# Softmax exponentials on VectorE: a cubic in four steps replaced by four integer mantissa readings that TensorE sums

## Chip, cores, metric

One core of a Trainium2 chip. The metric is the device time of one execution in microseconds (us). Every run lists the clock that TensorE was granted.

## The reference, cut to what matters

Two transformer layers, each an attention block and a feed-forward block, in bf16. Per layer 32 heads of width 16 look over 2048 tokens, so there are 2 x 32 x 2048 x 2048 exponentials. In tiles of 128 keys by 512 queries that is 4096 tiles. The two layers are the lines marked `A` below.

```python
def _A_ref(x, wqkv, wo):
    B, S, D = x.shape            # 1, 2048, 512
    H = 32; Dh = D // H
    ...
    scores = jnp.einsum("bhqd,bhkd->bhqk", q, k) * scale
    p = _softmax(scores, axis=-1)
    o = jnp.einsum("bhqk,bhkd->bhqd", p, v)
    ...
x = x + _A_ref(_layernorm(x, axis=-1), A_wqkv, A_wo)
x = x + _B_ref(_layernorm(x, axis=-1), B_w1, B_b1, B_w2, B_b2)   # gelu feed-forward, F = 1376
x = x + _A_ref(...); x = x + _B_ref(...)
```

## The kernel before: the parts that matter

The Python program is a list scheduler: it assigns each operation a guessed duration, decides in what order each engine gets its instructions, and writes that fixed order out with semaphores.

Scores come in groups of three and two tiles in turn (PSUM banks 0 to 2 and 3, 4), which ScalarE exponentiates with one instruction each. Beside a group, one more tile may go to bank 5 (`DLANE`), for VectorE:

```python
            grp = []
            while len(grp) < G:
                self.advance()
                if self.cur == len(self.segs):
                    break
                sg = self.segs[self.cur]
                grp.append((sg, sg["todo"].pop(0)))
            dt = self.take_d() if wide else None
            ...
            for k, (sg, j) in enumerate(grp + ([dt] if dt else [])):
                ops.append(self.score(sg, j, banks[k] if k < len(grp) else DLANE))
            ...
```

Whether there is such a tile is decided here; `lane_busy` is set when a tile is taken and cleared when its load out of bank 5 has been put into VectorE's order:

```python
    def take_d(self):

        self.advance()
        if self.lane_busy or self.cur == len(self.segs) or self.P.free["dve"] - self.S_.now > 1.3:
            return None
        ... (not in a segment's last DTAIL tiles; keys, queries there)
        if self.batch is None:
            p = self.S_.pools["dt"]
            if not p.free:
                return None
            self.batch = {"slot": p.free.pop(0), "tiles": [], "loaded": 0, "closed": False}
        self.lane_busy = True
        sg["todo"].pop(0)
        return (sg, j)

```

VectorE then computes the exponential of two tiles with four instructions, two of which read two tensors (`...` stands for their writes and guessed durations):

```python
    def job_d(self, bt):
        ...
        E,  in0=lo,  scalar=65536.0, in1=lo, op0=subtract, op1=mult        # scalar_tensor_tensor
        v,  in0=lo,  scalar1=..., scalar2=..., op0=mult, op1=add           # tensor_scalar
        D,  in0=E,   in1=v, op=mult                                        # tensor_tensor
        Pb, in0=t32, scalar=2.0 ** -9, in1=D, op0=mult, op1=subtract       # scalar_tensor_tensor
```

TensorE sums P·V of four heads at a time, in four column groups (`tile_position=(0, 32 * hp)`), and makes the scores in four row groups (`tile_position=(32 * hp, 0)`). Where the scheduler predicts a gap on TensorE of more than 0.35 us, it puts filler there, matmuls with zero weights, for 80% of the gap:

```python
FILL_GAP = 0.35
FILL_F = 0.8
    def fill_pe(self, gap):

        P = self.P
        t0 = P.free["pe"]
        n = int(FILL_F * (gap - 0.15) / FILL_T)
        if n < 1:
            return
        n = min(n, 60)
        ...
```

## Time and profile before

| | before |
|---|---|
| median of its runs | 1829.3 us (1827.3 to 1831.2) |
| ScalarE busy | 1741.9 us, 95% of the profiled span |
| VectorE busy | 1593.4 us, 87% |
| TensorE, filler included | 1702.4 us, 93% |
| tiles exponentiated by ScalarE / VectorE | 3635 / 461 |

How to read the lines in the prediction: a group's line names source line, engine, operation and shapes, then the count; after the first bar the busy time and the mean nanoseconds of one; after the second bar how long the engine stood idle just before them, and what ended that. The chain is followed back from the last instruction; its shares tell which engine's work or order set the end. In a view in order of time the first number is the start, the second the duration, and the bracket is an idle stretch and what ended it.

### The profile page before, as it was taken

To read this page: it belongs to the slowest core of one execution; us is meant where nothing else is said; L and a number is where in the kernel's file an instruction comes from. 1 tells how busy PE (TensorE), PEld (TensorE's weight loads), DVE (VectorE), ACT (ScalarE), POOL (GpSimd) and SP (SyncE) were. 2 spreads that over 40 slices of the span, in tenths; PEclk is the share of its full clock that TensorE was granted. 3 is DMA by queue.
4 is the path that set the end of the run, shared out by engine and by line. 5 is a ranking of instruction groups with operands and counts; after the bars stand their busy time and mean duration, and the time that the engine had idled before them with its cause. 6 is when DMAs were issued, how large, how long until landed. Compare 5 with 4: busy or idle time off the path is not lost.

```text
span 1827.5 us, 34039 instructions
## 1 busy us (share of the span) xinstructions
PE 1702.4 (93%) x13894; PEld 658.9 (36%) x13894; DVE 1593.4 (87%) x2516; ACT 1741.9 (95%) x1545; POOL 172.9 (9%) x328
## 2 busy tenths in 40 slices
PE   6989899999999999999999999999999999999998
PEld 2233333333333333333333333333333333333344
DVE  7789989997898999979988899887898798998885
ACT  5989999999999999999999999999999999999996
POOL 4122221100100110002000022100000000000000
PEclk9999999999999999999999999999999999999999
DMA  6551000100100110003500120000000000000000
GB/s 164 97 114 32 24 21 10 36 13 24 56 18 4 44 40 4 18 8 87 85 20 18 19 52 19 13 16 18 7 5 18 11 9 4 4 19 11 18 9 7
DMA packets 146400, 54.63 MB, mean 30 GB/s; under 512 B 131047, under 2 KB 140104, under 8 KB 146248
## 3 DMA queue, kind: packets, MB, share of 16 engines
q1 hardware_dynamic: 146248, 52.46, 12.6%
q8 instruction: 113, 1.85, 0.4%
q14 instruction: 39, 0.32, 0.1%
HBM read 8.69 MB, written 15.30 MB: 13 GB/s over the span
## 4 chain that ended last, share of the span: by engine, by line
ACT 58%; PE 34%; DVE 5%; DMA 2%; issue 1%; POOL 1%; SPq 0%; DVEq 0%; POOLq 0%
ACT PT L979 54%; PE ps L1005 10%; PE ps L1113 6%; PE ps L914 4%; PE ps L750 4%; PE ps L1235 3%; PE ps L1270 3%; PE ps L1203 3%; ACT h L1263 2%; DMA xnT<-xn 1%; DVE dt L990 1%; ACT L979 1%; ACT L1263 1%; DVE de L1064 1%; DVE de L1067 0%
## 5 line engine op out<-in xcount | busy, mean ns | idle before, releaser
L979 ACT ACTIVATE PT<-ps 128x1024 bf16<-128x1024 f32 (+1 forms) x1467 | 1666.2, 1287 | 52.8 <-PE ps L1005 48.5
L1005 PE MATMUL ps<-QT,KT 32*128 32x512 bf16 (+1 forms) x4608 | 605.3, 358 | 92.6 <-ACT PT L979 69.4
L914 PE MATMUL ps<-wqkv,zw 128*128 128x256 bf16 x3269 | 488.3, 276 | 0.0
L1113 PE MATMUL ps<-PT,V 128*17 128x512 bf16 (+1 forms) x4086 | 437.7, 361 | 3.6 <-DVE accT L1143 3.2
L990 DVE TENSOR_SCALAR dt<-ps 128x512 int32<-128x512 f32 x461 | 316.0, 686 | 135.1 <-PE ps L1005 131.7
L1005 PEld LDWEIGHTS ps<-QT,KT 32*128 32x128 bf16 x4608 | 171.8, 91 | 510.0 <-issue 295.3
L914 PEld LDWEIGHTS ps<-wqkv,zw 128*128 128x128 bf16 x3269 | 269.4, 98 | 196.2 <-issue 166.0
L1064 DVE SCALAR_TENSOR_TENSOR de<-dt 128x1024 bf16<-128x1024 uint16 (+1 forms) x243 | 282.2, 1163 | 2.1
L1067 DVE SCALAR_TENSOR_TENSOR de<-dt,dv 128x1024 uint16<-128x1024 int32 (+1 forms) x243 | 281.1, 1160 | 1.8
L1113 PEld LDWEIGHTS ps<-PT,V 128*17 128x17 bf16 x4086 | 108.9, 87 | 238.1 <-issue 204.1
L1066 DVE TENSOR_TENSOR dv<-de,dv 128x1024 f16<-128x1024 bf16 (+1 forms) x243 | 158.6, 655 | 2.0
L1065 DVE TENSOR_SCALAR dv<-dt 128x1024 bf16<-128x1024 uint16 (+1 forms) x243 | 159.7, 660 | 0.0
L1113 PE MATMUL ps<-de,V 128*17 128x512 bf16 (+1 forms) x522 | 137.3, 359 | 1.9 <-DVE accT L1143 0.9
L686 POOL TENSOR_SCALAR rs<-mv 128x4 f32<-128x4 f32 (+2 forms) x19 | 10.9, 572 | 967.1 <-DVE mv L679 966.8
L1235 PE MATMUL ps<-yT,w 128*128 128x512 bf16 (+3 forms) x396 | 97.1, 359 | 1.7 <-DMA yT<-xn 0.7
L750 PE MATMUL ps<-wqkv,xnT 128*128 128x512 bf16 x336 | 94.1, 386 | 4.6 <-DMA xnT<-xn 3.9
L1270 PE MATMUL ps<-w,h 128*128 128x512 bf16 x300 | 80.0, 382 | 0.4 <-ACT g L1264 0.2
L1143 DVE STREAM_TRANSPOSE accT<-ps 128x512 f32<-128x512 f32 (+1 forms) x88 | 58.3, 662 | 15.8 <-PE ps L1113 13.9
L1257 DVE TENSOR_SCALAR h<-ps,b1c 128x512 f32<-128x512 f32 (+2 forms) x88 | 61.8, 702 | 7.8 <-PE ps L1235 7.4
L1203 PE MATMUL ps<-wo,OT 128*128 128x512 bf16 x240 | 66.5, 383 | 0.2
L1183 DVE STREAM_TRANSPOSE OT<-ob 128x512 bf16<-128x512 bf16 (+1 forms) x72 | 46.0, 640 | 0.0
L1113 PEld LDWEIGHTS ps<-de,V 128*17 128x17 bf16 x522 | 32.2, 87 | 38.2 <-issue 29.5
(135 smaller groups left out, 768.8 us busy)
## 6 DMA issues: line engine op xcount, KB each, us to landing
q_scr<-qk SPq DMA_DIRECT2D x22, 256.0 KB, 2.0
k_scr<-qk SPq DMA_DIRECT2D x12, 256.0 KB, 2.0
q_scr<-h SPq DMA_DIRECT2D x10, 256.0 KB, 2.2
out_dram<-xres SPq DMA_DIRECT2D x16, 128.0 KB, 1.7
v_scr<-vst SPq DMA_DIRECT2D x12, 136.0 KB, 1.9
V<-v_scr SPq DMA_DIRECT2D x8, 204.0 KB, 4.6
wqkv<-in_A_wqkv_dram SPq DMA_DIRECT2D x3, 512.0 KB, 4.7
qraw<-q_scr SPq DMA_TRANSPOSE x87, 2.6
```

The lines of the kernel that those rows point to most:

```text
L750: yield Task("pe", prio, [I(lambda e, c=c: e.matmul(self.ps[:, b, :], lhsT=xnT[:, c, :], rhs=self.wqkv[:, c, which * 512:which * 512 + 512 ...
L914: P.op("pe", lambda e: e.matmul(self.ps[:, b, 0:w], lhsT=self.zw[:, :], rhs=rhs, start=st, stop=st, skip_group_check=True), [("zw",), R], ...
L979: S_.submit(Task("act", 1e-5 * gi, [I(lambda e, pt=pt, n=n, b0=b0: e.activation(out=self.PT[:, pt:pt + n, :], in_=self.ps[:, b0:b0 + n, :] ...
L990: S_.submit(Task("dve", 0.0, [I(lambda e, ds=ds, w=w: e.tensor_scalar(out=self.dt32[:, ds, w * 512:(w + 1) * 512], in0=self.ps[:, DLANE, : ...
L1005: return [I(lambda e, kb=kb, i=i: e.matmul(self.ps[:, b, i * W:(i + 1) * W], lhsT=self.KT[32 * hp:32 * hp + 32, hg, kb * 128:(kb + 1) * 12 ...
L1064: yield Task("dve", pr(), [I(lambda e: e.scalar_tensor_tensor(out=E, in0=lo, scalar=65536.0, in1=lo, op0=ALU.subtract, op1=ALU.mult), RT, ...
L1065: yield Task("dve", pr(), [I(lambda e: e.tensor_scalar(out=v, in0=lo, scalar1=CUB_B * sc / 65536.0, scalar2=CUB_A * sc, op0=ALU.mult, op1= ...
L1066: yield Task("dve", pr(), [I(lambda e: e.tensor_tensor(out=D, in0=E, in1=v, op=ALU.mult), [("de", es), ("dv", s)], [("dv", s)], 0.12 + 0.5 ...
L1067: yield Task("dve", pr(), [I(lambda e: e.scalar_tensor_tensor(out=Pb, in0=t32, scalar=2.0 ** -9, in1=D, op0=ALU.mult, op1=ALU.subtract), R ...
L1113: ops.append((i, I(lambda e, hp=hp, hg=hg, kb=kb, ap=ap[:, i * W:(i + 1) * W], first=first and i == 0, W=W: e.matmul(self.ps[32 * hp:32 * ...
L1235: yield Task("pe", pr, [I(lambda e, c=c: e.matmul(self.ps[0:M, b, off:off + W], lhsT=self.w1[:, c, fc * 128:fc * 128 + M], rhs=self.yT[:, ...
L1270: yield Task("pe", pr, [I(lambda e, fc=fc, i=i, b=b: e.matmul(self.ps[:, b, :], lhsT=self.gt(fc, i, W), rhs=self.w2[:, fc, :], start=(fc = ...
```

## The change

Its intent is to make a VectorE tile cheap. The bits of a bf16 number, read as an integer, are nearly linear in its logarithm; so adding a constant to the scaled score and storing it as a 16-bit integer gives a rough exponential, linear within each octave. The change makes four such readings, a quarter of an octave apart, and averages them: P·V is done once per reading, with copies of V multiplied by 1, 2^-1/4, 2^-1/2, 2^-3/4 (rounded). GpSimd makes the copies. To have them at hand, VectorE may only take five fixed key blocks of the 16. The space comes from the feed-forward buffer, f32 before and bf16 now.

```diff
-CUB_A = 38.926064531505304
-CUB_B = 10.143351058007678
+SHIFT = (0, 32, 64, 96)
+WSHIFT = (1.0, 0.83984375, 0.70703125, 0.59375)
+BITS0 = 127.0 * 128.0 - 263.2355
+DK = (3, 6, 9, 12, 15)
-DTAIL = 16
+DTAIL = 8
 ... (buffers: dp 3 x 4 x 1024 U16 and vs for dt32, dv, de; h16 for h32; one vst for two)
+    def job_vs(self, sg, i, kbs):          # GpSimd: weighted copies of V
+        ...
+        yield Task("pool", 0.8, [I(lambda e, k=k: e.tensor_scalar(out=self.vs[:, q, k - 1, i:i + n, :], in0=src, scalar1=WSHIFT[k], ...) for k in (1, 2, 3)])
 ...
-                grp.append((sg, sg["todo"].pop(0)))
+                grp.append((sg, (sg["todo"] or sg["todod"]).pop(0)))
 ...
-                ... tensor_scalar(out=self.dt32[...], in0=self.ps[:, DLANE, :], scalar1=512.0, scalar2=127.0 * 65536.0, op0=mult, op1=add)
+                ... tensor_scalar(out=self.dp[:, ds, 0, ...], in0=self.ps[:, DLANE, :], scalar1=BITS0, scalar2=None, op0=add)
 ... (take_d: from the list todod of the five key blocks)
-        j = sg["todo"][0]
+        j = sg["todod"][0]
+        sg["n"] += len(SHIFT) - 1
 ... (job_d: the four steps go)
+        for k in range(1, len(SHIFT)):
+            yield Task("dve", pr, [I(lambda e, k=k: e.tensor_scalar(out=self.dp[:, s, k, 0:N], in0=self.dp[:, s, 0, 0:N], scalar1=float(SHIFT[k]), scalar2=None, op0=ALU.add), ...)])
+            self.d_ready(bt, k, range(n))
 ... (P·V: the weighted copy where a reading k > 0 is summed)
+                    if sh:
+                        v, RV = self.vs[:, q, sh - 1, d, 17 * hp:17 * hp + 17], ("vs", q, d)
```

## The prediction

> **What bounds the kernel now.** I read the page's busy table first, then the costliest groups (with shapes kept apart), the chain that ended last, the list of waits, and two stretches of TensorE in order of time.
>
> ```profile
> PE 1702.4 (93%) x13894; PEld 658.9 (36%) x13894; DVE 1593.4 (87%) x2516; ACT 1741.9 (95%) x1545; POOL 172.9 (9%) x328
> ACT 58%; PE 34%; DVE 5%; DMA 2%; issue 1%; POOL 1%; SPq 0%; DVEq 0%; POOLq 0%
> ```
>
> ScalarE is busy 95% of the span, VectorE 87%. TensorE's 93% misleads, as the groups show; still, the chain (second line) runs through TensorE for 34% of the span, so TensorE's in-order stream is nearly co-critical.
>
> ```profile
> L979 ACT ACTIVATE PT<-ps 128x1536 bf16<-128x1536 f32 x701 | 1058.6, 1510 | 28.6 <-PE ps L1005 25.8
> L979 ACT ACTIVATE PT<-ps 128x1024 bf16<-128x1024 f32 x766 | 824.7, 1083 | 24.1 <-PE ps L1005 22.7
> L990 DVE TENSOR_SCALAR dt<-ps 128x512 int32<-128x512 f32 x461 | 316.0, 686 | 135.1 <-PE ps L1005 131.7
> L1064 DVE SCALAR_TENSOR_TENSOR de<-dt 128x1024 bf16<-128x1024 uint16 x218 | 265.0, 1216 | 2.0
> L1067 DVE SCALAR_TENSOR_TENSOR de<-dt,dv 128x1024 uint16<-128x1024 int32 x218 | 264.4, 1214 | 1.4
> L1065 DVE TENSOR_SCALAR dv<-dt 128x1024 bf16<-128x1024 uint16 x218 | 149.4, 687 | 0.0
> L1066 DVE TENSOR_TENSOR dv<-de,dv 128x1024 f16<-128x1024 bf16 x218 | 148.0, 680 | 1.7
> L914 PE MATMUL ps<-wqkv,zw 128*128 128x256 bf16 x3269 | 488.3, 276 | 0.0
> ```
>
> Softmax has 4096 score tiles of 128x512. ScalarE exponentiates 701x3 + 766x2 = 3635 of them, VectorE 461. The page gives the ScalarE line (forms together) 1666.2 us busy: 0.458 us a tile. A VectorE tile costs the load, 0.686, and four steps: on the page 282.2 + 281.1 + 159.7 + 158.6 = 881.6 us over 461 tiles, 1.91 us; together 2.60 us. That is 1198 of VectorE's 1593 us; 395 us is other work. L914 is filler, matmuls on zero weights put into predicted gaps; its 488 us is TensorE's slack.
>
> ```profile
> 909.64 0.27 PE L914 MATMUL ps<-wqkv,zw 128*128 128x256 bf16 x1
> 910.00 0.40 PE L1005 MATMUL ps<-QT,KT 32*128 32x512 bf16 x3
> 910.32 0.39 PE L1113 MATMUL ps<-PT,V 128*17 128x512 bf16 x4
> 910.91 0.39 PE L1005 MATMUL ps<-QT,KT 32*128 32x512 bf16 x2 [0.20 <-ACT PT L979]
> 911.24 0.94 PE L914 MATMUL ps<-wqkv,zw 128*128 128x256 bf16 x7
> ```
>
> A score group, whatever its two to four tiles, takes 0.32 to 0.33 us to the next start (910.00 to 910.32, 910.91 to 911.24); four P·V matmuls, one per column group, end as early. Adding start-to-start times by kind of run over the whole trace: scores 516 us (1440 runs, median 0.324), P·V 434 us (1021 runs; four matmuls median 0.328, eight 0.50), projections and feed-forward 341 us, filler 511 us.
>
> **What the Trainium skill says.** "VectorE: DVE Perf Modes", section "The perf-mode tier table": a tensor_scalar on 16-bit SBUF data reaches four elements a cycle, 32-bit half that, two-tensor ops less; the errata section of that page puts the fixed part near 150 cycles. The trace agrees for two a cycle: L1065 (16-bit input at step 2) has 687 ns at 1024 and 425 at 512 elements, 0.51 ns an element. The one dense 16-bit case:
>
> ```profile
> L877 DVE TENSOR_SCALAR QT<-qraw,scl,qbias 128x512 bf16<-128x512 bf16 x71 | 28.9, 410 | 2.4 <-DMA qraw<-q_scr 2.0
> L877 DVE TENSOR_SCALAR QT<-qraw,scl,qbias 128x256 bf16<-128x256 bf16 x16 | 5.0, 311 | 0.0
> ```
>
> Its lower tenths are 371 and 303 ns, 0.27 ns an element: four a cycle, with a larger fixed part[...]. "SBUF — State Buffer", section "Who interferes with whom": a two-port VectorE op and a GpSimd op exclude each other for the whole instruction. The trace agrees: the GpSimd 128x32 product at L815 has a median of 252 ns and a longest of 1114. "TensorEngine Tiling (Array Packing)", section "Key Properties": different tiles run in parallel, and a change of tiling mode drains the array. The trace agrees: four P·V matmuls in about 0.33 us, and some 0.23 us without a weight load at each change of kind.
>
> **The change part by part.**
> *VectorE.* Removed, per pair of tiles: two 1.216 us steps, a 0.687 and a 0.680. Added: three adds of a constant on dense 16-bit data, 128x1024. Estimate at four a cycle with 150 fixed cycles from the page above: (256 + 150)/0.96 = 423 ns. The load from PSUM stays at 0.686 (512 f32 from PSUM; its output type is not its limit). One tile: 0.686 + 3 x 0.423/2 = 1.32 us in place of 2.60.
> *ScalarE.* Each tile that moves to VectorE saves 0.458 us.
> *TensorE.* Each VectorE tile now needs four P·V matmuls, three more than before. Also, VectorE's key blocks now come from their own list, so a group's VectorE tile no longer takes the next head after the ScalarE tiles. Heads are row groups. With three ScalarE heads in use it meets one of them 3 times in 4, with two 2 in 4: about 0.625, each time some 0.2 us (one 512-column stream at the 8-against-4 step above, 0.50 - 0.33, rounded up), as the second matmul waits for its row group. The cost at build time is still 0.106 us a score.
> *GpSimd.* Three weighted copies of V for each of 80 segments; four small sets in the eight segments of layer 1's second part: about 312 instructions. With L686 near 0.2 us at 4 elements and L818 about 0.33 at 32 strided, I estimate 0.25 to 0.45 us each, about 110 us. POOL is at 9%; the sum is hidden. The lock may cost VectorE 10 to 40 us.
> *Feed-forward buffer.* Bias adds still read f32 from PSUM: about 0.74 to 0.69 us by comparison with the bf16 stores of that size, 4 us over 77. Gelu counts stay. Its purpose is room for the readings. One V staging buffer in place of two concerns 12 stores of 1.9 us: nothing.
>
> *How many tiles move.* Let n be VectorE's tiles and T the time. VectorE: 392 + 1.32 n. ScalarE: 1742 - 0.458 (n - 461). The cap is not near: five of 16 key blocks would allow about 1200, one tile a group about 1170. The third buffer and finer pieces should raise VectorE from 87% to about 90%, since little of its idle time is anything but the 132 us waiting for a score. ScalarE I lower from 95% to 92%, because TensorE gets tighter. Then (1953 - 0.458 n)/0.92 = (392 + 1.32 n)/0.90 gives n = 860, T = 1695.
> *TensorE at n = 860.* Groups: 3236 tiles/2.48 = 1306; scores 1306 x 0.358 = 468 us, plus collisions 860 x 0.625 x 0.2 = 108. P·V: 434 + 2580/4 x 0.25 (between a merged wave at 0.18 and one alone at 0.33) = 595. Other 341. Sum 1512 us, 89% of T, against 1291 of 1827 (71%) before. It fits if filler shrinks from 511 to below 180 us; it is tight.
>
> **The rivals.**
> 1. *TensorE becomes the bound.* The order is fixed at build time with no cost for collisions, and filler is put in where a gap is predicted. For: 34% of the chain already, and the sum above. Against: filler is 511 us of room, and two P·V waves together cost only 0.50. If 150 us of filler and another 80 us of switches remain, TensorE needs about 1740, T 1750 to 1790.
> 2. *The adds run at two a cycle* (0.69 us). One tile is then 1.72 us, and with the order fixed for shorter adds, 860 tiles need 392 + 1479 = 1871 us: T about 1930, slower. L877's slope speaks against it; that it is bf16 and not an integer type leaves a small chance.
> 3. *Buffers limit VectorE's share.* A buffer is now held from the first load until all four readings have gone through P·V, where before one was freed after the arithmetic. If this holds n to 650: ScalarE 1655/0.94 = 1761, still 3.7% faster. Early on only two are there.
> 4. *Everything lines up:* ScalarE stays at 95%, VectorE reaches 94%: n about 880, T about 1635.
>
> **Range and chances.** Predicted 1690 us, between the 1695 worked out and rival 4 with some weight on rival 1. The range 1610 to 1790 holds rivals 1, 3 and 4. Faster by over 2% means below 1793: 0.88. Within 2%: 0.07, for a worse rival 1. Slower: 0.05, for rival 2 or a segment's end waiting for late readings.
>
> **What would show it.** Right: the adds near 0.42 us; about 860 loads; ScalarE's exponentials near 1480 us; filler below half of 3269; P·V matmuls up by about half; ScalarE idle before exponentials up from 53 us to 100 or more, released by scores; score runs of 0.5 us where heads collide. Wrong: adds near 0.69; loads below 700; filler unchanged; the chain mostly on TensorE, with ScalarE below 88% (then rival 1); VectorE's waits on GpSimd over 50 us.

## The result and the profile after

1804.4 us (median of 4 runs, 1802.5 to 1808.5) against 1830.2 us of the kernel before beside it: a ratio of 0.9862, 95% interval 0.9839 to 0.9886. (A ratio is the mean time of one kernel's runs over that of the other's of the same rounds, so not quite the ratio of the medians quoted. Executions over 1.5% slower than the fastest of the same kernel are left out of the means.) The gain is 1.4%; 7.6% had been predicted, and the time lies above the predicted range.

First the busy table and the chain of the changed kernel:

```profile
PE 1715.9 (95%) x14796; PEld 598.0 (33%) x14930; DVE 1254.8 (70%) x2692; ACT 1679.4 (93%) x1478; POOL 380.2 (21%) x640
PE 64%; ACT 28%; DVE 4%; issue 2%; DMA 1%; POOL 1%; SPq 0%; POOLq 0%; DVEq 0%
```

VectorE fell from 87% to 70%, where about 90% was expected; ScalarE stands at 93%; and the chain now runs through TensorE for 64% of the span, 34% before. The costliest groups:

```profile
L1002 ACT ACTIVATE PT<-ps 128x1536 bf16<-128x1536 f32 (+1 forms) x1400 | 1603.8, 1250 | 90.5 <-PE ps L1028 82.9
L1013 DVE TENSOR_SCALAR dp<-ps 128x512 uint16<-128x512 f32 x628 | 431.0, 686 | 394.6 <-PE ps L1028 391.2
L905 POOL TENSOR_SCALAR vs<-V 128x340 bf16<-128x340 bf16 (+3 forms) x312 | 258.1, 834 | 1017.0 <-PE ps L1150 996.6
...
L1150 PE MATMUL ps<-dp,vs 128*17 128x512 bf16 (+1 forms) x2133 | 418.5, 357 | 0.4 <-DVE dp L1093 0.2
L1093 DVE TENSOR_SCALAR dp<-dp 128x1024 uint16<-128x1024 uint16 (+1 forms) x981 | 371.9, 425 | 6.5
L939 PE MATMUL ps<-wqkv,zw 128*128 128x256 bf16 x2172 | 321.6, 275 | 0.2 <-issue 0.2
...
L1150 PE MATMUL ps<-dp,V 128*17 128x512 bf16 (+1 forms) x711 | 194.2, 358 | 3.7 <-DVE accT L1176 2.9
```

Read from them: 628 loads (L1013), so ScalarE kept 3468 tiles. The added readings take 425 ns on average over two lengths; those of 1024 elements, estimated at 423 ns, have a median of 420 in the trace. VectorE stood idle 394.6 us before its loads, 391.2 of them for a score. ScalarE's exponentials are 62.4 us shorter (1666.2 to 1603.8). Its span outside busy time grew from 1827.5 - 1741.9 = 85.6 to 1802.8 - 1679.4 = 123.4 us. That is the whole account: 62.5 us less busy time, 38 more idle, 25 gained. (167 tiles at 0.458 us would have been 76 us; a tile that stayed now takes 0.462.) Filler shrank only from 3269 to 2172 matmuls.

The two waits behind this (us in total, how often, the longest):

```profile
DVE dp L1013 <- PE ps L1028: 391.2, 382, 9.2
...
ACT PT L1002 <- PE ps L1028: 82.9, 164, 6.4
```

TensorE in order of time, from the middle of the changed kernel:

```profile
904.84 0.39 PE L1028 MATMUL ps<-QT,KT 32*128 32x512 bf16 x2
905.15 0.83 PE L939 MATMUL ps<-wqkv,zw 128*128 128x256 bf16 x6
905.95 0.40 PE L1028 MATMUL ps<-QT,KT 32*128 32x512 bf16 x4
...
906.87 0.39 PE L1028 MATMUL ps<-QT,KT 32*128 32x512 bf16 x2
...
910.47 0.59 PE L1028 MATMUL ps<-QT,KT 32*128 32x512 bf16 x4
910.99 0.38 PE L1150 MATMUL ps<-PT,V 128*17 128x512 bf16 x1
```

The groups at 904.84 and 906.87 have two tiles and none for VectorE; those at 905.95 and 910.47 have four, three for ScalarE and one for VectorE. Only every second group carries a VectorE tile. At 910.47 the group takes 0.52 us to the next start instead of the usual 0.32: two of its four heads share a row group. VectorE in the same stretch:

```profile
901.94 0.69 DVE L1013 TENSOR_SCALAR dp<-ps 128x512 uint16<-128x512 f32 x1 [0.44 <-PE ps L1028]
904.17 0.69 DVE L1013 TENSOR_SCALAR dp<-ps 128x512 uint16<-128x512 f32 x1 [1.53 <-PE ps L1028]
904.89 1.10 DVE L1093 TENSOR_SCALAR dp<-dp 128x1024 uint16<-128x1024 uint16 x3
906.46 0.69 DVE L1013 TENSOR_SCALAR dp<-ps 128x512 uint16<-128x512 f32 x1 [0.47 <-PE ps L1028]
```

It loads a tile, has little else, and waits for the next: 2.2 us from load to load, two group times.

### The profile page after: what moved, and what is told of

Same layout as the page of the kernel before. It is cut to its first block, busy times and chain, and to the rows that moved or that the text cites. A ratio compares the mean times of both kernels' runs of the same rounds, so it can differ in the third digit from the quotient of the medians.

```text
span 1802.8 us, 36197 instructions
## 1 busy us (share of the span) xinstructions
PE 1715.9 (95%) x14796; PEld 598.0 (33%) x14930; DVE 1254.8 (70%) x2692; ACT 1679.4 (93%) x1478; POOL 380.2 (21%) x640
## 4 chain that ended last, share of the span: by engine, by line
PE 64%; ACT 28%; DVE 4%; issue 2%; DMA 1%; POOL 1%; SPq 0%; POOLq 0%; DVEq 0%
ACT PT L1002 24%; PE ps L1028 21%; PE ps L1150 20%; PE ps L939 8%; PE ps L761 5%; PE ps L1268 4%; PE ps L1303 3%; PE ps L1236 3%; ACT h L1296 2%; DVE dp L1093 1%; DVE dp L1013 1%; ACT L1002 1%; ACT L1296 1%; POOL vs L905 1%; DMA xnT<-xn 0%
## 5 line engine op out<-in xcount | busy, mean ns | idle before, releaser
L1002 ACT ACTIVATE PT<-ps 128x1536 bf16<-128x1536 f32 (+1 forms) x1400 | 1603.8, 1250 | 90.5 <-PE ps L1028 82.9
L1013 DVE TENSOR_SCALAR dp<-ps 128x512 uint16<-128x512 f32 x628 | 431.0, 686 | 394.6 <-PE ps L1028 391.2
L1150 PE MATMUL ps<-PT,V 128*17 128x512 bf16 (+1 forms) x3897 | 557.5, 359 | 0.4 <-ACT PT L1002 0.3
L905 POOL TENSOR_SCALAR vs<-V 128x340 bf16<-128x340 bf16 (+3 forms) x312 | 258.1, 834 | 1017.0 <-PE ps L1150 996.6
L1150 PE MATMUL ps<-dp,vs 128*17 128x512 bf16 (+1 forms) x2133 | 418.5, 357 | 0.4 <-DVE dp L1093 0.2
L1093 DVE TENSOR_SCALAR dp<-dp 128x1024 uint16<-128x1024 uint16 (+1 forms) x981 | 371.9, 425 | 6.5
L939 PE MATMUL ps<-wqkv,zw 128*128 128x256 bf16 x2172 | 321.6, 275 | 0.2 <-issue 0.2
L939 PEld LDWEIGHTS ps<-wqkv,zw 128*128 128x128 bf16 x2172 | 179.3, 98 | 150.6 <-issue 132.1
L1150 PE MATMUL ps<-dp,V 128*17 128x512 bf16 (+1 forms) x711 | 194.2, 358 | 3.7 <-DVE accT L1176 2.9
L1150 PEld LDWEIGHTS ps<-dp,vs 128*17 128x17 bf16 x2133 | 99.3, 88 | 163.9 <-issue 150.9
L1290 DVE TENSOR_SCALAR h<-ps,b1c 128x512 bf16<-128x512 f32 (+2 forms) x88 | 62.5, 710 | 25.9 <-PE ps L1268 24.7
```

Source lines behind the costliest of these rows:

```text
L905: yield Task("pool", 0.8, [I(lambda e, k=k: e.tensor_scalar(out=self.vs[:, q, k - 1, i:i + n, :], in0=src, scalar1=WSHIFT[k], scalar2=None ...
L939: P.op("pe", lambda e: e.matmul(self.ps[:, b, 0:w], lhsT=self.zw[:, :], rhs=rhs, start=st, stop=st, skip_group_check=True), [("zw",), R], ...
L1002: S_.submit(Task("act", 1e-5 * gi, [I(lambda e, pt=pt, n=n, b0=b0: e.activation(out=self.PT[:, pt:pt + n, :], in_=self.ps[:, b0:b0 + n, :] ...
L1013: S_.submit(Task("dve", 0.0, [I(lambda e, ds=ds, w=w: e.tensor_scalar(out=self.dp[:, ds, 0, w * 512:(w + 1) * 512], in0=self.ps[:, DLANE, ...
L1093: yield Task("dve", pr, [I(lambda e, k=k: e.tensor_scalar(out=self.dp[:, s, k, 0:N], in0=self.dp[:, s, 0, 0:N], scalar1=float(SHIFT[k]), s ...
L1150: ops.append((i, I(lambda e, hp=hp, v=v, ap=ap[:, i * W:(i + 1) * W], first=first and i == 0, W=W: e.matmul(self.ps[32 * hp:32 * hp + 17, ...
```

## Experiments

Times are medians; "before" beside them was 1828 to 1831 us. TensorE's times by kind of work are start-to-start sums over its whole trace, as in the prediction: changed kernel 560 scores, 578 P·V, 317 other (the trace lost some of its matmuls), 323 filler; before 516, 434, 341, 511.

### 1. One P·V matmul in place of four

Only the first reading is summed; VectorE still makes the others and GpSimd its copies.

```diff
+BITS0 = 127.0 * 128.0 - 7.35
-        sg["n"] += len(SHIFT) - 1
-            self.d_ready(bt, k, range(n))
```

> The changed kernel with the three added readings still computed by VectorE and the weighted copies of V still made by GpSimd, but only the first reading sent through P·V (wrong weights of the exponential on purpose, bias constant adapted). VectorE tiles stay about the same (639 loads in the program against 628). Theory T, that TensorE's in-order stream holds ScalarE up: about 1880 P·V matmuls fall away, ScalarE's idle time before exponentials goes from 90 us back to 55 or less, time 1740 to 1765. Theory V, that the missing VectorE tiles alone explain the small gain: TensorE was not in the way, time 1795 to 1805.

1765.1 us, ratio 0.9654. Its chain and exponentials:

```profile
ACT 46%; PE 40%; DVE 8%; DMA 3%; POOL 2%; issue 1%; POOLq 0%; DVEq 0%; SPq 0%
...
L1002 ACT ACTIVATE PT<-ps 128x1536 bf16<-128x1536 f32 (+1 forms) x1396 | 1590.1, 1279 | 65.7 <-PE ps L1028 59.9
```

ScalarE's idle time before exponentials falls from 90.5 to 65.7 us (55 or less had been expected), and the chain goes back to ScalarE. P·V took 414 us in place of 578. The time came out at the slow edge of what theory T said: the three further matmuls a tile cost the changed kernel 39 us, of which some 5 are 11 tiles that this order happened to move as well (11 x 0.46). The weights were wrong, and yet the result passed the comparison with the reference.

### 2. Heads that do not meet, and its control

VectorE's tile is picked so that its head is not among those of its group.

```diff
-            dt = self.take_d() if wide else None
+            dt = self.take_d({sg["tiles"][j][1] for sg, j in grp}) if wide else None
-        j = sg["todod"][0]
+        j = next((j for j in sg["todod"] if sg["tiles"][j][1] not in used), sg["todod"][0])
```

With this the scheduler ran into a dead end, so two rules were mended: a half-filled buffer is closed once its segment has passed, and P·V may go with fewer than four heads when ScalarE waits for output buffers. The control has these mends alone.

> The changed kernel, but VectorE's tile is chosen from its list so that its head (row group) is not among those of the ScalarE tiles of the same group; 629 VectorE tiles. Theory T with collisions as a main part of TensorE's extra load: score runs of 4 with a median of 0.53 us go back to 0.33, TensorE saves up to 80 us of stream, time 1765 to 1785. Rival: collisions sit in what would be filler or waiting anyway, time 1797 to 1808. The kernel also has a small mend of two rules in the schedule (closing a half-filled buffer, P·V going early when ScalarE's output buffers have run out), without which it cannot be scheduled; alone they are expected to be worth under 5 us.

> Control for the run with other heads: the changed kernel with only the two small mends of the schedule. 628 VectorE tiles as in the changed kernel. Expected by all theories: within 6 us of the changed kernel's 1804; if it is at 1776 the heads had nothing to do with that run's gain.

Other heads: 1776.1 us, ratio 0.9717. The control: 1802.2 us, ratio 0.9860. So collisions cost 26 us, and the mends nothing that can be told. The score matmuls of the control, then of the run with other heads:

```profile
L1029 PE MATMUL ps<-QT,KT 32*128 32x512 bf16 (+1 forms) x4608 | 638.3, 359 | 35.5 <-ACT PT L1002 24.6
```

```profile
L1029 PE MATMUL ps<-QT,KT 32*128 32x512 bf16 (+1 forms) x4608 | 551.7, 359 | 54.5 <-ACT PT L1002 39.6
```

These lines are busy times with overlaps taken out, for the same 4608 matmuls. Start to start, scores fell from 549 to 461 us, by 88 us. P·V rose from 569 to 605 us in the same pair of traces, so not all of the 88 us became free.

### 3. The feed-forward buffer alone

In the kernel before, the buffer is written as bf16, nothing else.

```diff
-        hv = self.h32[:, :, :].rearrange("p f n -> p (f n)")
+        hv = self.gv
```

> The kernel before with the feed-forward buffer in bf16 alone (the space is not used). All theories: bias adds stay near 0.74 us, the in-place Gelu near 4.47 us; time within 4 us of the kernel before.

1831.8 us, ratio 1.0015 (1.0000 to 1.0029). This part gives space and no time.

### 4. Two VectorE tiles outstanding on the one bank

The first attempt let `lane_busy` count to two.

```diff
-        if self.lane_busy or self.cur == len(self.segs) or ...
+        if self.lane_busy >= LANES or self.cur == len(self.segs) or ...        # LANES = 2
```

> The changed kernel, but a VectorE tile may be put into the next score group while the load of the one before is still to be done (two outstanding on the one PSUM bank in place of one); the program then has 776 VectorE tiles in place of 628, with the same two small mends as in the run with other heads. Theory L, that the single outstanding tile is what kept VectorE at 628 tiles and that tiles are worth 0.46 us of ScalarE each: 148 tiles, 68 us, time 1735 to 1750. Theory T, that TensorE is the bound by now: 444 more P·V matmuls and more collisions eat it, ScalarE's share falls below 91%, time 1785 to 1815.

1814.2 us, and a wrong result (relative error 0.11): a tile's score could be put into the order ahead of the load of the tile before, and overwrote bank 5. The order itself was wrong. The second attempt, with heads as in experiment 2, was wrong too (relative error 0.19):

> Both together, mended: up to two VectorE tiles outstanding, the second one's score in a TensorE task of its own that is put behind the load before it (in the earlier run with two outstanding the score could be put in ahead of that load, and overwrote the bank: that is why it was wrong), and heads that do not meet those of the group. 766 VectorE tiles. If collisions were what turned more tiles into a loss: time 1735 to 1765, ScalarE near 1620 us busy at 92% or more. If the four P·V matmuls per tile alone are enough to make TensorE the bound: 1775 to 1815, the chain over 55% on TensorE. The result should be correct.

It had put about half of VectorE's scores into no order at all (its trace has 4128 score matmuls in place of 4608), so its 1742.1 us is not evidence. A version with one reading and the same fault (3889 score matmuls, relative error 0.21, 1590.4 us) falls with it:

> A version that the first runs point to: one reading a tile (which passed the comparison with 639 tiles), no further adds, one P·V matmul a tile, two tiles outstanding, heads that do not collide. 991 VectorE tiles, so ScalarE has 530 fewer than in the kernel before, 243 us. VectorE falls to about 65%. With TensorE's stream no longer than before the change: time 1590 to 1650. If a longer TensorE stream is not what matters, it gains only what ScalarE's share of the changed kernel gives: 1640 to 1680. Whether the result stays within tolerance with 991 tiles is open.

The third attempt gives a tile whose bank is still occupied a score task of its own, which waits until the load before it is in the order:

```diff
+            scored = bool(dt) and ("dl", self.nd) in S_.done
-            for k, (sg, j) in enumerate(grp + ([dt] if dt else [])):
+            for k, (sg, j) in enumerate(grp + ([dt] if scored else [])):
+    def job_dl(self, dt, bt, w, k, scored):
+        if not scored:
+            yield ("keys", [("dl", k)])
+            yield Task("pe", 0.0, self.score(dt[0], dt[1], DLANE))
+        ... the load; then S_.mark(("dl", k + 1))
```

> Two VectorE tiles outstanding, now with every score in the program and in the right place (the first attempt overwrote scores; in the second, with other heads, about half of VectorE's scores were missing from the program, so its 1742 us is not to be used). 770 VectorE tiles, heads as in the changed kernel. Theory L (tiles alone are missing): 142 tiles x 0.46 = 65 us, 1735 to 1750. Theory T (TensorE's stream is the bound): 426 more P·V matmuls and more collisions take it back, 1785 to 1820, ScalarE at 91% or less, the chain over 60% on TensorE. Result correct.

> The same with heads that do not meet those of the group; 762 VectorE tiles. Theory T with collisions removed: 1745 to 1775, between the run with other heads alone (1776) and theory L's 1740. If the four P·V matmuls per tile alone saturate TensorE: no better than 1776. Result correct.

Both are correct. Two outstanding, heads as in the change: 770 tiles, 1804.4 us, ratio 0.9857, the same as the changed kernel. With heads that do not meet: 762 tiles, 1797.6 us, ratio 0.9818, and so 21 us slower than with 629 tiles (experiment 2); of the two forecasts, "no better than 1776" held. The chain and the exponentials of the latter:

```profile
PE 73%; ACT 18%; DVE 5%; POOL 2%; DMA 1%; issue 1%; SPq 0%; DVEq 0%; POOLq 0%
...
L1005 ACT ACTIVATE PT<-ps 128x1536 bf16<-128x1536 f32 (+1 forms) x1347 | 1547.8, 1241 | 134.0 <-PE ps L1029 126.9
```

So the one outstanding tile is what kept VectorE at 628: with two, 770 went over. But those tiles bought nothing: ScalarE's exponentials went down to 1547.8 us and its idle time before them up to 134.0. Two things cloud this test. A score in a task of its own is often a run of its own: 188 runs have one score, none in experiment 2. And such a score can land beside a group that uses its head: heads meet again in some 170 runs (a score starting over 0.12 us after the one before it), against some 20 in experiment 2. Scores took 552 us, 91 more than there. The experiment lifts the limit at a price on TensorE; whether a second bank, without that price, would do better is not shown, since all eight banks are in use.

### 5. One reading and nothing else of the four

No further adds, no copies of V, one P·V matmul, heads that do not meet, one tile outstanding (655 tiles).

```diff
+SHIFT = (0,)
+BITS0 = 127.0 * 128.0 - 7.35
-        if sg["dks"] and not (L == 1 and ...):
+        if len(SHIFT) > 1 and sg["dks"] and not (L == 1 and ...):
```

> One reading a tile and nothing else of the four (no further adds, no weighted copies, no P·V for them), one tile outstanding, heads that do not collide: 655 VectorE tiles. Against the run with one P·V alone (1765) it has no collisions, no GpSimd copies and a VectorE at about half: theory T 1725 to 1745. If after the P·V matmuls nothing more was in the way: 1755 to 1765.

1724.0 us, ratio 0.9421, correct, just below the 1725 to 1745 that were expected. Busy table and exponentials:

```profile
PE 1571.8 (91%) x13350; PEld 594.0 (35%) x13350; DVE 930.7 (54%) x1738; ACT 1650.8 (96%) x1467; POOL 117.0 (7%) x328
...
L1002 ACT ACTIVATE PT<-ps 128x1536 bf16<-128x1536 f32 (+1 forms) x1389 | 1575.6, 1310 | 37.5 <-PE ps L1029 33.4
```

ScalarE is back at 96%. This is 80 us under the changed kernel with only 27 tiles more. The parts add up roughly: 39 for P·V (experiment 1), 26 for collisions (experiment 2), and 655 - 639 = 16 tiles x 0.46 = 7; 8 us are left for the adds, the copies and what the parts do to each other.

### 6. Filler

TensorE's filler had been booked as slack in the prediction. Both runs have the mends of the control.

```diff
-FILL_F = 0.8
+FILL_F = 0.0        # and 0.4 in the second
```

> The changed kernel with the two mends and no filler at all (2172 matmuls on zero weights less, order otherwise the same). If filler placed by the schedule's too low TensorE costs is in the way: 10 to 30 us faster than the control. If TensorE only loses waiting time by it: same as the control within 6 us. If the clock falls because TensorE then idles more: slower, with a granted clock below 0.97.

> The changed kernel with the two small mends and half the filler (935 matmuls on zero weights in place of 2093; without any the clock fell to 0.81). If filler that the schedule places by too low TensorE costs is what fills TensorE: 10 to 30 us faster than the control's 1802 with the clock above 0.98. If the real work of TensorE is what matters: 1795 to 1805. If the clock falls below 0.96: slower.

Without filler 1939.4 us (ratio 1.0596), with half of it 1826.1 (ratio 0.9979), against 1802.2. The granted clock in 40 slices, in tenths, without filler and then with half:

```profile
PEclk7968557889688876998779895787888986878879
```

```profile
PEclk8879999999999999999999989899999999989969
```

The mean granted clock is 0.81 and 0.961; it is 0.995 in the control. In the trace with half the filler TensorE never stands still for more than 2.9 us between the start and the tail, and still 143 us of it ran at half rate. The same for the kernel with two tiles outstanding and heads that do not meet:

> The kernel with two tiles outstanding and heads that do not collide (1797.6) with less than half of its filler (741 in place of 1661). In that kernel scores, P·V and other matmuls take 1517 of 1791 us, 85%, filler the rest. If filler is what is left over at TensorE's expense: 1745 to 1780. If P·V in the order laid down is: 1790 to 1800. If the clock suffers: slower than 1800.

1805.9 us with clocks of 0.970 to 0.975, against 1797.6 with 0.996 to 0.998.

### 7. An order made with measured durations

Score groups are booked at 0.324 us, 0.21 more where heads meet, a single score at 0.30, an added reading at 0.42, a copy of V by its length (1.06 us for five blocks).

```diff
+            t = 0.324 + (0.21 if len(set(hps)) < len(hps) else 0.0)
+            ops = [o[:4] + (t / len(ops),) + o[5:] for o in ops]
-                                     ... 0.1 + 0.26e-3 * N)])
+                                     ... 0.155 + 0.26e-3 * N)])
-                                     ... 0.15 + 0.06 * n, ...
+                                     ... 0.21 + 0.17 * n, ...
```

> The same kernel (full filler rule), but the order is made with the durations that the traces show: a score group 0.324 us and 0.21 more where heads meet, a VectorE tile's score alone 0.30, an added reading 0.42, a weighted copy of V 1.06. 736 VectorE tiles, 1157 filler matmuls. If too low costs make the order bad: 1730 to 1770. If the P·V work itself is too much for TensorE: 1785 to 1800.

1787.8 us, ratio 0.9775 (0.9734 to 0.9816), inconclusive: filler fell with the predicted gaps, and the clock with it. Its four runs went with the clock: 1771.2 us at 0.985, 1781.9 at 0.978, 1793.6 and 1795.3 at 0.969. So the filler was brought back (`FILL_F = 1.2`, order otherwise made the same way):

> The kernel of g_lane2priced (order made with the measured durations) with its filler brought back: each predicted gap filled to 120% in place of 80%, 1874 filler matmuls in place of 1157; 724 VectorE tiles. If the clock (0.969 to 0.985 there) is what cost g_lane2priced its gain: clock 0.99 or more and 1745 to 1770. If filler only takes TensorE's time: 1785 to 1810.

1771.3 us, ratio 0.9678 over its three runs at 0.994 to 0.998 (a fourth was slow: 1808.5 at 0.972), about 1 us above the forecast of 1745 to 1770. So both counted, the order and the clock: with true prices, and filler enough to hold the clock, 724 tiles with four readings come to 26 us less than the 762 of experiment 4. Still, that is only 5 us less than the 629 tiles of experiment 2. An order with one tile outstanding was not made again with true prices.

### 8. Versions that beat both kernels

Experiment 5 with two tiles outstanding, 950 of them:

> The version that the runs point to, all scores in place: one reading, two outstanding, heads that do not collide, no weighted copies; 950 VectorE tiles. ScalarE's exponentials (4096 - 950) x 0.46 = 1447 us. With TensorE's P·V no longer than before the change: 1595 to 1650. If TensorE still holds it: 1650 to 1700. Correctness with 950 tiles of one reading is open: one reading passed with 639.

1669.4 us, ratio 0.9116, correct; it lies in the range given for TensorE still holding it. In its trace heads meet again in some 300 runs and scores take 601 us, 465 in experiment 5: the pick falls back to any head when none is free, and a score of its own can land beside its head. With the measured durations of experiment 7 it has 903 tiles and less filler:

> The fast version (one reading, two outstanding, heads that do not collide, 1669 us) with the same durations for its order; 903 VectorE tiles, 1339 filler matmuls in place of 1988. If the order is what holds it above the 1620 that ScalarE's share would allow: 1630 to 1655. If not: 1665 to 1680, as it has 47 tiles fewer.

1730.0 us at a clock of 0.91 to 0.92, ratio 0.9439: worse, where both forecasts (1630 to 1655, 1665 to 1680) had it near or below the version before. The clock is the reason that the next run tests. With the filler brought back:

> The same for the version with one reading: 903 VectorE tiles, 1965 filler matmuls in place of 1339. If the clock (0.91 to 0.92 there) is what cost it: clock 0.98 or more and 1635 to 1665. If not: 1690 to 1730.

1655.8 us, ratio 0.9065 (0.9005 to 0.9125), correct, at a clock of 0.972 to 0.991. Its busy table:

```profile
PE 1578.8 (95%) x12590; PEld 552.3 (33%) x12590; DVE 1086.6 (66%) x1986; ACT 1543.6 (93%) x1368; POOL 116.3 (7%) x328
```

That is the fastest correct version: one reading a tile, 903 tiles, 9.4% under the kernel before. Its tolerance is a matter of this comparison alone; it has no averaging over four readings.

## Why the prediction was wrong, point by point

**The step that failed first: "How many tiles move".** The prediction took n from two fill levels, VectorE at 90% and ScalarE at 92%, and got 860; it said that "the cap is not near", with one tile a group. The run has 628, about one in every second group. The tile for a group is chosen when the group before it has just gone to TensorE, and then bank 5 still waits to be read. The trace agrees (628 loads in 1400 groups, 391 us of VectorE waiting for scores), and experiment 4 shows that this rule is the limit: with two outstanding there are 770. Put n = 628 into the prediction's own formula, (1953 - 0.458 x 628)/0.92, and it gives 1810 us; 1804 was measured. The term that was mis-sized is the 399 tiles that should have moved: 167 did. ScalarE's share, 92% predicted, was 93%. This step alone does not explain the time, though: with 762 tiles the formula gives 1743 us, and 1797.6 were measured (experiment 4).

**The second step that failed: "It fits if filler shrinks".** The prediction called filler TensorE's slack. Its sum of TensorE's own work was good for the changed kernel: with 628 tiles it gives 1472 us, and 560 + 578 + 317 = 1455 were measured. It did not hold for more tiles: for 762 without collisions it gives 1399 us, and experiment 4 shows 552 + 620 + 345 = 1517, with 249 us of filler besides. Experiment 6 shows in the changed kernel that halving filler costs 24 us, with the clock at 0.961, and removing it 137, with the clock at 0.81. So room that filler takes is not free for P·V. That is rival 1 ("TensorE becomes the bound") with a reason that the prediction did not have; its range of 1750 to 1790 was also too low. Of its signs, the chain on TensorE came (64%), ScalarE below 88% did not (93%). Taking work off TensorE at nearly the same number of tiles gave 39, 26 and 80 us (experiments 1, 2 and 5). It also holds back what more tiles could give (experiment 4), though part of the loss there is that experiment's own extra score runs. With one reading more tiles do pay, if less than 0.46 us each: 1669.4 us with 950 against 1724.0 with 655.

**Collisions: right.** Predicted at 0.2 us each and 108 us of TensorE for 860 tiles, thus 79 for 628; measured 0.52 against 0.32 us for a group, and 88 us of scores between control and experiment 2. The prediction did not say what it would cost at the end: 26 us of time.

**P·V: mis-sized a little.** Predicted 0.25 us for a wave of four; the 2133 further matmuls cost 578 - 414 = 164 us, 0.31 us a wave. Many waves are runs of their own: P·V has 1232 runs, 952 in experiment 1. At the end they cost 39 us of time.

**VectorE: right, but its time no longer sets the number of tiles.** The readings at 423 ns: a median of 420 measured, so rival 2 is out. A tile costs about 0.686 + 1.5 x 0.425 = 1.32 us, half of before, and yet VectorE ended at 70%, waiting for scores. The lock with GpSimd had been put at 10 to 40 us: 183 of the readings of 1024 elements ran beside a GpSimd instruction and took 499 ns on average, the other 720 took 419, so 15 us in all. (The 1114 ns that the prediction shows for L815 came beside steps with two tensor inputs; beside L1065 that product took 579 to 582.)

**Buffers (rival 3): not the cause at 628.** Lifting the outstanding limit with the same three buffers brought 142 tiles more. What holds 770 is open.

**GpSimd: over twice the estimate, hidden.** 258 us in place of 110. The estimate came from small operations, and one was misread: L686, put near 0.2 us, has 193 ns only as its shortest and a median of 547. With copies and adds gone as well, 8 us stay unexplained in experiment 5, so their cost in time is at most about that; this is argued, not shown.

**Feed-forward buffer: right that it gives room, wrong in its 4 us.** The bias adds were to become faster; they stayed as slow as before (0.735 us before, 0.743 after), and the time did not change (experiment 3).

**A slip in rival 4.** Its two fill levels, 95% and 94%, meet at 869 tiles and 1637 us, not at 880 and 1635.

## What to carry to other kernels

Before counting what a cheaper operation on a second engine will take over, find the rule that hands it work: here one PSUM bank, held from choice to load, allowed one tile in two groups whatever a tile cost. Work that is moved between two engines by giving a third engine, TensorE, more matmuls has to be paid in that engine's fixed order, and filler that keeps its clock up is not slack. Where a result tolerates it, the cheapest reading (one, not four) was worth more than its refinement.

## What the Trainium skill lacked or had wrong

- "TensorE: Matmul & The Clock Gate", section "Why this matters for your kernels", asks for no idle gaps over some 3 us between bursts of matmuls. Taken alone, that was not enough here: with half the filler the longest gap between the first 100 us and the tail was 2.9 us, and 143 us of the trace ran at half rate (mean clock 0.961, 1826.1 against 1802.2 us). The page also tells of short idle stretches between groups of matmuls after which the clock swung, but not how much of a window small tiled matmuls fill, or that matmuls on zero weights hold the clock (0.995 with 2093 of them, 0.81 with none).
- "TensorEngine Tiling (Array Packing)", section "Key Properties", says that tiles work in parallel and that a change of mode drains the array, without numbers. Here four matmuls in four row groups take 0.325 us to the next kind of run (the median in experiment 2), and 0.534 (the median in the changed kernel) where mostly two of them share a row group. We found figures for tiles in parallel on another page of the skill, none for two matmuls of one row group.
- "GPSIMD Engine Reference", section "Elementwise — side-by-side cycle accounting", gives about 2.6 cycles an element, for a sum of two f32 tensors, and its section "Engine selection" calls one input roughly line-rate. Here a bf16 tensor_scalar, which has one input, took a median of 1061 ns at 340 elements and 380 at 68: 2.5 ns an element, 3.0 cycles at that page's 1.2 GHz.
